# Retention attention into a SoLU block on one core: where q is transposed, how g_ln is loaded, and how the last 512 tokens are laid out

## The chip, the cores and the metric

The kernel runs on one core of one Trainium2 chip. The metric is the device time of one execution in microseconds (us), lower is better. The core has a matrix engine (PE, fed with weights by PEld), a vector engine (DVE), an activation engine (ACT), GpSimd (POOL) and a sync engine (SP) that only issues transfers. Sixteen DMA engines move data between HBM and the on-chip memory SBUF; matrix results land in the eight banks of PSUM.

## The reference

```python
kv  = einsum('bhsd,bhse->bhde', k, v)            # b=8, h=8, s=576, d=64: no softmax
o   = einsum('bhsd,bhde->bhse', q, kv)
o   = o / sqrt(mean(o*o, -1) + 1e-6) * g_norm    # norm over the 64 values of a head
x   = o.transpose(0, 2, 1, 3).reshape(4608, 512)
hid = x @ w_in                                   # 512 -> 1024
e   = exp(hid - max(hid));  u = hid * e / (sum(e) + 1e-9)
ln  = (u - mean(u)) / sqrt(var(u) + 1e-6) * g_ln # over the 1024 values of a token
out = ln @ w_out                                 # 1024 -> 512, float32
```

## The kernel before

The 4608 tokens are worked off in nine **chunks** of 512. Chunk c below 8 is the first 512 tokens of batch c; a partition p holds the four tokens 4p to 4p+3 (the groups j). Chunk 8 takes the last 64 tokens of all eight batches: partition 16b+p holds four tokens of batch b. Everything is computed with features on the partitions and tokens on the free axis, in bf16 where it feeds PE.

A chunk passes these steps. `kv_mm` (L272) makes k'v per head in a PSUM bank of the tag `misc`, four copies (L282 on DVE, L284 on ACT, one after the other) bring it to `kvd`. q is transposed to `qT`: in the chunks of `XBAR` by one DMA through the crossbar (`q_turn`, L302, issued by SP), in the others by 16 PE transposes in two halves (`qT_mm`, L292, also in a `misc` bank, of which there is one) with a DVE copy for each half (L297). `o_mm` (L317) gives the attention output in two halves of heads `hf`, each in two banks z. Each of the four pieces is squared (L332 on ACT; or copied by DVE, L324, and squared by L328), averaged per head by `s_mm` (L338), turned into 1/rms by a logarithm and an exponential (L342, L346), and multiplied in (`x_mul`, L353), which frees the `o` bank. Then eight tiles f of `h_mm` (L420, four matmuls each), each followed by the exponential `e` (L428), the product `u` (L435, which frees one of two `h` banks), its square `usq` (L444 on ACT, L446 on POOL) and the sums of pairs of `e` (`es`, L452 on POOL). `sums` (L484) adds u, u² and e over the features by PE, DVE transposes the result (L493), a small matmul (L498) and four small DVE instructions give the variance, two on ACT `rstd` (L518, L520). The mean of a token is taken out of `w_out` beforehand: `w_mean` (L526, eight matmuls in float32) and `w_center` (L532, eight DVE instructions) make `w_out_sb` once, in chunk 0. Last, `out_mm` (L541, four groups m of eight matmuls), `scale` by rstd (L548, `ob`) and `store` (L557, 256 KB each).

POOL issues all loads (L210 k and v, L217 q, L223 the last tokens of q, L230, L233 the weights); these cast float32 to bf16 on the way. Three buffers each hold k, v and q, so loads run up to three chunks ahead. SP issues the small loads at the start, the crossbar transposes and the stores; the last chunk's odd stores go out from ACT's queue. `warm` (L186) is a set of matmuls on zeros between the first real ones.

The order on every engine is made at build time by `Plan.order`: each step has an engine, an assumed length, a rank and what it needs; again and again the step that could start first goes next, the rank breaks ties. Each engine then works strictly in that order, waiting by semaphore. Numbers in `plan.add` thus set an order and no times.

Of the kernel before, what the change touches and what calls it, by code (L numbers as in the profile page):

```python
# [84 lines left out]
def kernel(  # L85
# [20 lines left out]
    nc = tc.nc  # L106
# [13 lines left out]
    XBAR = tuple(range(3, NC))  # L120
# [11 lines left out]
    COPIED = (0,)  # L132
# [15 lines left out]
    nc.sync.dma_start(g_ln_sb[:, :], moe_g_ln.rearrange("(n p) -> p n", p=128))  # L148

    ident = big.tile([128, 128], BF16, name="ident")  # L150
    fold = big.tile([128, 32], FP32, name="fold")
# [303 lines left out]
    for c in range(NC):  # L455
        for f in range(NF):
# [9 lines left out]
            engine = "act" if f in (2, 6) and c > 1 else "pool"  # L466
# [98 lines left out]
    for c in range(NC):  # L565
# [10 lines left out]
        for m in range(4):  # L576
# [7 lines left out]
            plan.add(("ob", c, m), "dve", 0.67, r + (2 * m + 2) / 8, lambda c=c, m=m: scale(c, m),  # L584
# [36 lines left out]
```

## Time and profile before

| | |
|---|---|
| median of 3 runs | 211.62 us (210.85 to 212.26) |
| the profiled execution | 212.84 us |
| its span, first to last instruction | 211.1 us |
| PE, DVE, ACT, POOL busy | 186.9, 128.5, 133.0, 135.5 us |
| mean granted clock of PE | 0.971 of full speed |

The profile is of one execution; its views are a page of sums, windows (busy time of each engine in a stretch), the chain that ended last, and a timeline of single instructions. A time in brackets at a row's end is the idle time of that engine just before, with what ended it. Starts are exact; the ends of matmuls are modelled, so PE work is best measured from start to start.

### The profile page before, as it was taken

The numbers are of one execution on the slowest core, as the hardware profiler recorded it, in microseconds if no ns is written. First come the engines' busy times: TensorE is split into PE (matmuls) and PEld (weight loads), VectorE is DVE, ScalarE is ACT, GpSimd is POOL, SyncE is SP. The second block draws the span as 40 slices with busy tenths as digits, with TensorE's granted clock in tenths as the row PEclk, the third lists the DMA queues.
The fourth block names the chain that finished last, engine by engine and source line by source line (L and its number), as shares of the span: only waits on it lengthen the run. The fifth ranks groups of instructions, "written<-read, shape, count | busy, mean of one in ns | idle before, by whom it ended". The sixth has DMA issues, their size and how long they took to land.

```text
span 211.1 us, 4084 instructions
## 1 busy us (share of the span) xinstructions
PE 186.9 (89%) x1614; PEld 83.2 (39%) x1614; DVE 128.5 (61%) x243; ACT 133.0 (63%) x231; POOL 135.5 (64%) x142
## 2 busy tenths in 40 slices
PE   7499897889948999999999999999999999999900
PEld 2243442543412435435444443543444444444300
DVE  1444567579860759667676866858666577663420
ACT  2046599456842877969779796976978585353100
POOL 7772389994380788696796966569385568586000
PEclk9999999999995999999999999999999999999995
DMA  4999999999999239979999997662121022022042
GB/s 47 163 203 205 199 373 227 200 202 203 193 123 237 64 33 195 242 121 148 237 176 128 212 248 112 204 107 104 50 102 50 25 78 90 14 97 101 0 115 83
DMA packets 43058, 30.14 MB, mean 143 GB/s; under 512 B 14880, under 2 KB 37408, under 8 KB 43040
## 3 DMA queue, kind: packets, MB, share of 16 engines
q0 software_dynamic: 24208, 17.30, 54.2%
q1 hardware_dynamic: 18560, 12.07, 22.4%
q10 hardware_dynamic: 272, 0.52, 0.8%
q8 instruction: 12, 0.20, 0.4%
q14 instruction: 6, 0.05, 0.1%
HBM read 32.51 MB, written 9.44 MB: 199 GB/s over the span
## 4 chain that ended last, share of the span: by engine, by line
PE 64%; DMA 25%; DVE 3%; issue 1%; ACT 1%; POOL 0%; DVEq 0%; POOLq 0%
PE out_ps L541 27%; PE h_ps L420 24%; DMA q_sb<-in_q_dram 9%; DMA v_sb<-in_v_dram 7%; DMA qT_sb<-q_sb 6%; PE misc_ps L484 5%; DMA k_sb<-in_k_dram 3%; PE s_ps L338 3%; PE o_ps L317 2%; DVE w_out_sb L532 2%; PE misc_ps L272 2%; PE misc_ps L498 1%; DVE ob_sb L548 1%; PE misc_ps L292 1%; POOL q_sb L217 0%
## 5 line engine op out<-in xcount | busy, mean ns | idle before, releaser
L420 PE MATMUL h_ps<-x_sb,w_in_sb 128*128 128x512 bf16 x288 | 74.7, 383 | 0.5 <-DVE u_sb L435 0.4
L541 PE MATMUL out_ps<-w_out_sb,u_sb 128*128 128x512 bf16 x272 | 70.6, 384 | 0.4 <-DVE w_out_sb L532 0.3
L452 POOL TENSOR_TENSOR es_sb<-e_sb 128x512 bf16<-128x512 f32 x36 | 45.8, 1272 | 36.5 <-ACT e_sb L428 36.3
L446 POOL TENSOR_TENSOR usq_sb<-u_sb 128x512 bf16<-128x512 bf16 x58 | 59.9, 1038 | 13.7 <-DVE u_sb L435 9.2
L435 DVE TENSOR_TENSOR u_sb<-h_ps,e_sb 128x512 bf16<-128x512 f32 x72 | 49.4, 687 | 31.6 <-ACT e_sb L428 30.9
L428 ACT ACTIVATE e_sb<-h_ps,zero_t 128x512 f32<-128x512 f32 x72 | 49.3, 684 | 21.2 <-PE h_ps L420 20.8
L541 PEld LDWEIGHTS <-u_sb 128*128 128x128 bf16 x288 | 27.2, 99 | 34.9 <-issue 5.6
L420 PEld LDWEIGHTS <-w_in_sb 128*128 128x128 bf16 x288 | 27.2, 98 | 34.5 <-issue 5.4
L548 DVE TENSOR_SCALAR ob_sb<-out_ps,rstd 128x512 f32<-128x512 f32 x34 | 25.2, 745 | 10.7 <-PE out_ps L541 6.8
L332 ACT ACTIVATE osq_sb<-o_ps,zero_t 128x512 bf16<-128x512 f32 x31 | 19.7, 682 | 14.6 <-PE o_ps L317 14.5
L353 DVE SCALAR_TENSOR_TENSOR x_sb<-o_ps,g_rep,rst_sb 128x512 bf16<-128x512 f32 x32 | 23.9, 747 | 7.8 <-ACT rst_sb L346 7.8
L346 ACT ACTIVATE rst_sb<-lss_sb,zero_t 128x512 f32<-128x512 f32 x36 | 26.1, 725 | 0.6
L342 ACT ACTIVATE lss_sb<-s_ps,eps_t 128x512 f32<-128x512 f32 x34 | 23.4, 688 | 1.5 <-PE s_ps L338 1.3
L284 ACT CAST kvd<-misc_ps 64x256 bf16<-64x256 f32 (+1 forms) x20 | 6.5, 325 | 14.6 <-DVE kvd L282 13.9
L338 PE MATMUL s_ps<-osq_sb,head_mean 128*128 128x512 bf16 x34 | 13.2, 388 | 0.9 <-ACT lss_sb L342 0.5
L186 PE MATMUL s_ps<-zeros 128*128 128x512 bf16 x39 | 11.6, 427 | 1.5 <-DVE zeros L153 1.2
L317 PE MATMUL o_ps<-qT_sb,kvd 64*64 64x32 bf16 (+1 forms) x240 | 7.7, 232 | 4.2 <-DMA qT_sb<-q_sb 4.1
L444 ACT ACTIVATE usq_sb<-u_sb,zero_t 128x512 bf16<-128x512 bf16 x14 | 10.1, 720 | 0.9 <-DVE u_sb L435 0.9
L217 POOL DMA_DIRECT2D q_sb<-in_q_dram x10 | 8.7, 872 | 2.2 <-DMA v_sb<-in_v_dram 1.4
L272 PE MATMUL misc_ps<-v_sb,k_sb 96*64 96x64 bf16 x384 | 8.0, 197 | 2.1 <-DMA v_sb<-in_v_dram 2.1
L210 POOL DMA_DIRECT2D k_sb<-in_k_dram x10 | 7.6, 760 | 3.3 <-DMA w_in_sb<-in_moe_w_in_dram 2.7
L518 ACT ACTIVATE lv<-vare,zero_t 128x4 f32<-128x4 f32 x9 | 2.7, 297 | 10.9 <-DVE vare L514 10.9
(60 smaller groups left out, 123.8 us busy)
## 6 DMA issues: line engine op xcount, KB each, us to landing
out_dram<-ob_sb SPq DMA_DIRECT2D x34, 256.0 KB, 3.1
k_sb<-in_k_dram POOLq DMA_DIRECT2D x6, 576.0 KB, 9.0
v_sb<-in_v_dram POOLq DMA_DIRECT2D x6, 576.0 KB, 12.5
q_sb<-in_q_dram POOLq DMA_DIRECT2D x6, 512.0 KB, 15.0
w_out_f<-in_moe_w_out_dram POOLq DMA_DIRECT2D x1, 2048.0 KB, 18.1
k_sb<-in_k_dram POOLq DMA_DIRECT2D x4, 288.0 KB, 11.0
v_sb<-in_v_dram POOLq DMA_DIRECT2D x4, 288.0 KB, 11.4
q_sb<-in_q_dram POOLq DMA_DIRECT2D x4, 256.0 KB, 10.5
```

The source lines that it names most:

```text
L332: nc.scalar.activation(out=t[:, :], in_=T[("o", *i)].rearrange("p a b c -> p (a b c)"), func=AF.Square, bias=zero_t[:, :])
L338: nc.tensor.matmul(t[:, :], head_mean[:, :], T["osq", i][:, :], start=True, stop=True)
L342: nc.scalar.activation(out=t[:, :], in_=T["s", i][:, :], func=AF.Ln, bias=eps_t[:, :])
L346: nc.scalar.activation(out=t.rearrange("p a b c -> p (a b c)"), in_=T["lss", i][:, :], func=AF.Exp, scale=-0.5, bias=zero_t[:, :])
L353: nc.vector.scalar_tensor_tensor(out=T["x", c][:, 2 * hf:2 * hf + 2, z], in0=T["o", c, hf, z][:, :, :, :], scalar=g_rep[:, :], in1=T["rst" ...
L420: nc.tensor.matmul(t[:, :], w_in_sb[:, dt, f * 128:(f + 1) * 128], T["x", c][:, dt].rearrange("p a b c -> p (a b c)"), start=(dt == 0), st ...
L428: nc.scalar.activation(out=T["e", c, f // 2][:, f % 2, :], in_=T["h", c, f][:, :], func=AF.Exp, bias=zero_t[:, :])
L435: nc.vector.tensor_tensor(out=T["u", c][:, f, :], in0=T["h", c, f][:, :], in1=T["e", c, f // 2][:, f % 2, :], op=MUL)
L446: nc.gpsimd.tensor_tensor(out=dst, in0=src, in1=src, op=MUL)
L452: nc.gpsimd.tensor_tensor(out=T["es", c][:, n, :], in0=e[:, 0, :], in1=e[:, 1, :], op=ADD)
L541: nc.tensor.matmul(T["acc", c, m][:, :], T["u", c][:, f, m * 128:(m + 1) * 128], w_out_sb[:, f, :], start=(f == 0), stop=(f == NF - 1),)
L548: nc.vector.tensor_scalar_mul(out=t[:, :], in0=T["acc", c, m][:, :], scalar1=T["rstd", c][:, m:m + 1])
```

## The change

Six edits stand in it. The crossbar takes chunks 4 to 8, so that chunk 3 goes by PE and DVE. g_ln (1024 floats) is loaded as eight rows of 128 and turned by one PE transpose, where it was loaded as 128 columns of eight single floats. In chunk 8 the partition is 8p+b in place of 16b+p: the load of the last q, the columns in `o_mm` and the pattern of the stores follow. Of the squares that go by a copy, chunk 0 keeps one (first half) and chunk 1 gets two, all three on POOL now. In chunk 8, ACT takes five of the eight u² and two of the four last scales. The warm matmuls go from 54 to 40. The planner's table changes with it.

```diff
-    XBAR = tuple(range(3, NC))
+    XBAR = tuple(range(4, NC))
...
-    COPIED = (0,)
+    COPIED = ((0, 0), (1, 0), (1, 1))
...
-    nc.sync.dma_start(g_ln_sb[:, :], moe_g_ln.rearrange("(n p) -> p n", p=128))
+    g_rows = big.tile([NF, 128], FP32, name="g_rows")
+    nc.sync.dma_start(g_rows[:, :], moe_g_ln.rearrange("(n p) -> n p", p=128))
...
+    def turn_g():
+        t = T["g_ps"] = bank(("misc", "g"), [128, NF], FP32)
+        nc.tensor.transpose(t[:, :], g_rows[:, :], eye[:NF, :NF])
+
     def make_g_mean():
+        nc.vector.tensor_copy(g_ln_sb[:, :], T["g_ps"][:, :])
...
-    for n in range(9):
-        plan.add(("warm", "s", n), "pe", 0.65, 8.0, lambda: warm(3), ["warm"], first=[("s", "warm", n)])
-    for n, key in enumerate((("o_mm", 0, 1), ("s_mm", (0, 0, 0)), ("s_mm", (0, 1, 0)), ("s_mm", (0, 0, 1)), ("s_mm", (0, 1, 1)))):
-        plan.add(("warm", n), "pe", 0.7, -9.0, lambda: warm(3, "misc"), [key], first=[("misc", "warm", n)])
+    for n in range(8):
+        plan.add(("warm", "s", n), "pe", 0.45, 8.0, lambda: warm(2), ["warm"], first=[("s", "warm", n)])
+    for n, key in enumerate((("o_mm", 0, 0), ("s_mm", (0, 0, 0)), ("o_mm", 0, 1), ("s_mm", (0, 1, 0)))):
+        plan.add(("warm", n), "pe", 0.65, 7.0, lambda: warm(3, "misc"), [key], first=[("misc", "warm", n)])
...
-            q_last[16 * b:16 * b + 16].rearrange("p h j d -> p h (j d)"),
+            q_last[b:128:B].rearrange("p h j d -> p h (j d)"),
...
-                cols = slice(0, 128) if c < B else slice(16 * b, 16 * b + 16)
+                cols = slice(0, 128) if c < B else slice(b, 128, B)
...
-        (nc.vector if i[1] else nc.gpsimd).tensor_tensor(out=t[:, :], in0=T["oc", i][:, :], in1=T["oc", i][:, :], op=MUL)
+        nc.gpsimd.tensor_tensor(out=t[:, :], in0=T["oc", i][:, :], in1=T["oc", i][:, :], op=MUL)
...
-            engine = "act" if f in (2, 6) and c > 1 else "pool"
+            engine = "act" if f in ((2, 6) if c < NC - 1 else (1, 3, 5, 6, 7)) and c > 1 else "pool"
...
-        nc.vector.tensor_scalar_mul(out=t[:, :], in0=T["acc", c, m][:, :], scalar1=T["rstd", c][:, m:m + 1])
+        if c == NC - 1 and m % 2:
+            nc.scalar.activation(out=t[:, :], in_=T["acc", c, m][:, :], func=AF.Copy, scale=T["rstd", c][:, m:m + 1])
+        else:
+            nc.vector.tensor_scalar_mul(out=t[:, :], in0=T["acc", c, m][:, :], scalar1=T["rstd", c][:, m:m + 1])
...
-            dst = out.rearrange("(b s) d -> b s d", b=B)[:, 512:S, :].rearrange("b (p j) d -> j b p d", j=4)
+            dst = out.rearrange("(b s) d -> b s d", b=B)[:, 512:S, :].rearrange("b (p j) d -> j p b d", j=4)
```

The order moves at three places that matter below. The first is DVE in chunk 2, around `w_center`; `x_sb_747` (before) and `x_sb_745` (changed) are the pieces of chunk 2, `u_sb_624` and `u_sb_573` those of chunk 1. Before:

```order
L435 TENSOR_TENSOR u_sb_624<-h_ps_630,e_sb_572 128x512
L297 COPY qT_sb_659<-misc_ps_641 128x1024
L532 SCALAR_TENSOR_TENSOR w_out_sb_69<-w_out_f_68,g_ln_sb_73,out_ps_555 128x512 x2
L297 COPY qT_sb_659<-misc_ps_670 128x1024
L532 SCALAR_TENSOR_TENSOR w_out_sb_69<-w_out_f_68,g_ln_sb_73,out_ps_555 128x512 x6
L353 SCALAR_TENSOR_TENSOR x_sb_747<-o_ps_681,g_rep_72,rst_sb_737 128x2x256
L493 STREAM_TRANSPOSE sumT_sb_753<-misc_ps_697 128x512
L353 SCALAR_TENSOR_TENSOR x_sb_747<-o_ps_682,g_rep_72,rst_sb_745 128x2x256
L435 TENSOR_TENSOR u_sb_624<-h_ps_652,e_sb_666 128x512
```

The same place on DVE in the changed kernel:

```order
L306 COPY qT_sb_651<-misc_ps_639 128x1024
L444 TENSOR_TENSOR u_sb_573<-h_ps_631,e_sb_648 128x512
L541 SCALAR_TENSOR_TENSOR w_out_sb_69<-w_out_f_68,g_ln_sb_73,out_ps_547 128x512
L306 COPY qT_sb_651<-misc_ps_663 128x1024
L541 SCALAR_TENSOR_TENSOR w_out_sb_69<-w_out_f_68,g_ln_sb_73,out_ps_547 128x512 x5
L362 SCALAR_TENSOR_TENSOR x_sb_745<-o_ps_675,g_rep_72,rst_sb_727 128x2x256
L541 SCALAR_TENSOR_TENSOR w_out_sb_69<-w_out_f_68,g_ln_sb_73,out_ps_547 128x512 x2
L362 SCALAR_TENSOR_TENSOR x_sb_745<-o_ps_676,g_rep_72,rst_sb_741 128x2x256
L502 STREAM_TRANSPOSE sumT_sb_758<-misc_ps_699 128x512
```

Both pieces of x now stand ahead of the transpose of the sums, one of them between the last two `w_center` and the rest. The second place is DVE a little later, where chunk 3 begins (the `CAST` to `kvd_70` are its kv copies). Before:

```order
L353 SCALAR_TENSOR_TENSOR x_sb_747<-o_ps_769,g_rep_72,rst_sb_861 128x2x256
L282 CAST kvd_70<-misc_ps_798 64x256 x2
L435 TENSOR_TENSOR u_sb_624<-h_ps_856,e_sb_877 128x512
L353 SCALAR_TENSOR_TENSOR x_sb_747<-o_ps_770,g_rep_72,rst_sb_889 128x2x256
L435 TENSOR_TENSOR u_sb_624<-h_ps_883,e_sb_877 128x512
L548 TENSOR_SCALAR ob_sb_907<-out_ps_872,rstd_849 128x512
L435 TENSOR_TENSOR u_sb_624<-h_ps_898,e_sb_919 128x512
```

The same place on DVE in the changed kernel:

```order
L362 SCALAR_TENSOR_TENSOR x_sb_745<-o_ps_760,g_rep_72,rst_sb_856 128x2x256
L291 CAST kvd_70<-misc_ps_807 64x256 x2
L560 TENSOR_SCALAR ob_sb_880<-out_ps_771,rstd_805 128x512
L362 SCALAR_TENSOR_TENSOR x_sb_745<-o_ps_761,g_rep_72,rst_sb_882 128x2x256
L306 COPY qT_sb_901<-misc_ps_884 128x1024
L444 TENSOR_TENSOR u_sb_573<-h_ps_875,e_sb_721 128x512
L560 TENSOR_SCALAR ob_sb_909<-out_ps_865,rstd_805 128x512
L306 COPY qT_sb_901<-misc_ps_911 128x1024
```

Two copies to `qT_sb_901`, chunk 3's, have come in between. The third place is the end of ACT's program. Before:

```order
L428 ACTIVATE e_sb_2748<-h_ps_2752,zero_t_83 128x512
L518 ACTIVATE lv_2832<-vare_2830,zero_t_83 128x4
L520 ACTIVATE rstd_2834<-lv_2832,zero_t_83 128x4
L557 DMA out_0_dram<-ob_sb_2847 8x16x512
L557 DMA out_0_dram<-ob_sb_2853 8x16x512
```

The end of ACT's program in the changed kernel:

```order
L453 ACTIVATE usq_sb_2641<-u_sb_2639,zero_t_85 128x512
L527 ACTIVATE lv_2842<-vare_2840,zero_t_85 128x4
L529 ACTIVATE rstd_2844<-lv_2842,zero_t_85 128x4
L558 ACTIVATE ob_sb_2852<-out_ps_2819,rstd_2844 128x512
L569 DMA out_0_dram<-ob_sb_2852 16x8x512
L558 ACTIVATE ob_sb_2868<-o_ps_2854,rstd_2844 128x512
L569 DMA out_0_dram<-ob_sb_2868 16x8x512
```

ACT scales two of the four last results itself and issues their stores, whose pattern now begins with 16 in place of 8. On SP the first crossbar transpose, chunk 3's, falls away, and the next one (chunk 4) stands between the second and the third store as before. On PE 16 transposes come in ahead of chunk 3's `o_mm`, and the last `sums` stands four `out` matmuls earlier. From the second `sums` to the last chunk the order on all engines is nearly the one before.

## Rows read from the trace of the kernel before

**Rows 1.** The page: busy time by engine; PE's granted clock in 40 slices (tenths).

```profile
PE 186.9 (89%) x1614; PEld 83.2 (39%) x1614; DVE 128.5 (61%) x243; ACT 133.0 (63%) x231; POOL 135.5 (64%) x142
...
PEclk9999999999995999999999999999999999999995
```

**Rows 2.** The chain that ended last: start, length, what (us).

```profile
51.41 12.79 DMA qT_sb<-q_sb
64.23 0.64 PE o_ps L317 x8
...
69.93 0.86 PE h_ps L420 x4
...
84.72 0.34 PE o_ps L317 x8
...
87.97 0.86 PE h_ps L420 x4
```

**Rows 3.** Windows: stretch, its length, busy time (instructions) by engine, clock, DMA.

```profile
core 0: us, PE busy (x) PEld busy (x) DVE busy (x) ACT busy (x) POOL busy (x), PEclk, DMA share, GB/s
23.60:43.30 19.70, 16.14 (x162) 7.92 (x155) 12.02 (x22) 14.84 (x28) 16.81 (x17) 1.00 1.35 254
43.30:60.20 16.90, 15.81 (x157) 7.44 (x157) 15.12 (x28) 12.03 (x21) 9.38 (x11) 1.00 1.35 196
60.20:64.20 4.00, 0.00 (x0) 0.00 (x0) 1.86 (x4) 0.69 (x1) 3.15 (x3) 0.77 1.20 125
64.20:69.20 5.00, 4.97 (x19) 1.84 (x20) 0.04 (x1) 2.02 (x4) 0.00 (x0) 0.50 0.82 203
```

**Rows 4.** Timeline of PE: q transposes of chunk 2, `o_mm` of chunk 3.

```profile
43.30 0.62 PE L292 MATMUL misc_ps<-ident,q_sb 128*128 128x128 bf16 x8 [0.57 <-DMA q_sb<-in_q_dram]
...
45.80 0.61 PE L292 MATMUL misc_ps<-ident,q_sb 128*128 128x128 bf16 x8
...
64.23 0.64 PE L317 MATMUL o_ps<-qT_sb,kvd 64*64 64x256 bf16 x8 [4.07 <-DMA qT_sb<-q_sb]
```

**Rows 5.** Timeline of DVE and POOL, single instructions of the fill.

```profile
12.78 0.68 DVE L324 COPY oc_sb<-o_ps 128x512 f32<-128x512 f32 x1
...
13.93 1.05 POOL L328 TENSOR_TENSOR osq_sb<-oc_sb 128x512 bf16<-128x512 f32 x1
...
41.51 2.03 POOL L446 TENSOR_TENSOR usq_sb<-u_sb 128x512 bf16<-128x512 bf16 x2
...
46.44 0.69 DVE L297 COPY qT_sb<-misc_ps 128x1024 bf16<-128x1024 bf16 x1 [0.17 <-PE misc_ps L292]
...
47.05 4.03 DVE L532 SCALAR_TENSOR_TENSOR w_out_sb<-w_out_f,g_ln_sb,out_ps 128x512 bf16<-128x512 f32 x6
```

**Rows 6.** Windows as in rows 3: start, an ordinary store, the last stores, the end.

```profile
4.50:7.50 3.00, 2.12 (x16) 1.01 (x15) 0.78 (x2) 0.00 (x0) 3.00 (x5) 1.00 1.08 115
7.50:14.30 6.80, 4.97 (x54) 2.10 (x53) 3.42 (x9) 1.79 (x4) 4.03 (x7) 1.00 1.31 194
194.00:194.50 0.50, 0.50 (x4) 0.24 (x3) 0.00 (x0) 0.00 (x0) 0.50 (x1) 1.00 0.98 377
203.50:204.00 0.50, 0.00 (x0) 0.00 (x0) 0.00 (x0) 0.00 (x0) 0.00 (x0) 1.00 0.53 193
209.60:211.10 1.50, 0.00 (x0) 0.00 (x0) 0.00 (x0) 0.00 (x0) 0.00 (x0) 0.50 0.00 0
```

**Rows 7.** Timeline of the last instructions on PE, DVE and ACT's queue.

```profile
197.90 2.76 PE L541 MATMUL o_ps<-w_out_sb,u_sb 128*128 128x512 bf16 x12
...
200.64 1.40 DVE L548 TENSOR_SCALAR ob_sb<-o_ps,rstd 128x512 f32<-128x512 f32 x2
...
200.75 1.94 ACTq L557 DMA_DIRECT2D out_dram<-ob_sb  x2
```

**Rows 8.** DMA issues of 190 to 196 us: median us from issue to landing.

```profile
out_dram<-ob_sb SPq DMA_DIRECT2D x2, 256.0 KB, 2.3
```

**Rows 9.** Timeline of PE: one half of chunk 8's `o_mm`.

```profile
155.82 0.69 PE L317 MATMUL o_ps<-qT_sb,kvd 64*64 64x32 bf16 x64
```

More of the change, by code (lines that the diff above doesn't have):

```diff
@@ L147 @@
     nc.sync.dma_start(g_rep[64:128, :], g_norm[:, None])
-    nc.sync.dma_start(g_ln_sb[:, :], moe_g_ln.rearrange("(n p) -> p n", p=128))
+    g_rows = big.tile([NF, 128], FP32, name="g_rows")
+    nc.sync.dma_start(g_rows[:, :], moe_g_ln.rearrange("(n p) -> n p", p=128))
     ident = big.tile([128, 128], BF16, name="ident")
+    eye = big.tile([NF, NF], FP32, name="eye")
     fold = big.tile([128, 32], FP32, name="fold")
@@ L177, in make_g_mean @@
         )
-    plan.add("g_mean", "dve", 1.2, 0.1, make_g_mean)
+    plan.add("turn_g", "pe", 0.2, -1.9, turn_g, ["ident"], first=[("misc", "g")])
+    plan.add("g_mean", "dve", 0.95, 0.1, make_g_mean, ["turn_g"], uses=[("misc", "g")])
     def warm(n, tag="s"):
@@ L188 @@
     plan.add("warm", "pe", 5.2, -9.0, lambda: warm(12), first=[("s", "warm")])
-    for n in range(9):
-        plan.add(("warm", "s", n), "pe", 0.65, 8.0, lambda: warm(3), ["warm"], first=[("s", "warm", n)])
-    for n, key in enumerate((("o_mm", 0, 1), ("s_mm", (0, 0, 0)), ("s_mm", (0, 1, 0)), ("s_mm", (0, 0, 1)), ("s_mm", (0, 1, 1)))):
-        plan.add(("warm", n), "pe", 0.7, -9.0, lambda: warm(3, "misc"), [key], first=[("misc", "warm", n)])
+    for n in range(8):
+        plan.add(("warm", "s", n), "pe", 0.45, 8.0, lambda: warm(2), ["warm"], first=[("s", "warm", n)])
+    for n, key in enumerate((("o_mm", 0, 0), ("s_mm", (0, 0, 0)), ("o_mm", 0, 1), ("s_mm", (0, 1, 0)))):
+        plan.add(("warm", n), "pe", 0.65, 7.0, lambda: warm(3, "misc"), [key], first=[("misc", "warm", n)])
     def make_ident():
         make_identity(nc, ident)
+        make_identity(nc, eye)
     def make_fold():
@@ L395 @@
                 rz = r + w * (0.4 + 0.5 * hf + 0.12 * z)
-                if c in COPIED and z:
+                if (c, hf) in COPIED and z:
                     plan.add(("oc", i), "dve", 0.62, rz, lambda i=i: o_copy(*i), [("o_mm", c, hf)],
                              uses=[(tag, *i)], first=[("oc", i)])
-                    plan.add(("sq", i), "dve" if hf else "pool", 0.62 if hf else 1.3, rz + 0.01, lambda i=i: o_sq_copy(*i), [("oc", i)],
+                    plan.add(("sq", i), "pool", 1.05, rz + 0.01, lambda i=i: o_sq_copy(*i), [("oc", i)],
                              uses=[("oc", i)], first=[("osq", i)])
@@ L583 @@
                          uses=[("u", c)] + ([(tag, c, m)] if half else []), first=[] if half else [(tag, c, m)])
-            plan.add(("ob", c, m), "dve", 0.67, r + (2 * m + 2) / 8, lambda c=c, m=m: scale(c, m),
+            plan.add(("ob", c, m), "act" if c == NC - 1 and m % 2 else "dve", 0.67, r + (2 * m + 2) / 8, lambda c=c, m=m: scale(c, m),
                      [("out", c, m, 1), ("rstd", c)], uses=[(tag, c, m)], first=[("ob", c, m)])
```

## The prediction

> **What bounds the kernel now.** I read the page first. PE is busy for 186.9 of 211.1 us, and the row of its granted clock has one dip ahead of the end, in the 13th of 40 slices, at 63 to 69 us [rows 1]. So PE is the bound, but not everywhere, and the question is where it waits. The chain that ended last answers: from about 70 us to 199 us it is PE work without a break, and what interrupts PE is ahead of that and behind it [rows 2]. There are three places.
>
> The first is the stall of chunk 3. SP issues its crossbar transpose at 51.41 us, as soon as q has landed, and it takes 12.79 us, since the loads of chunk 4 run beside it [rows 2]. PE has nothing else in its order and idles for 4.07 us [rows 4]. PE's clock goes down in this idle time (mean 0.77, then 0.50, that is 1.2 of 2.4 GHz) and stays down to about 69 us [rows 3]. Its price is read off the chain: the same five groups (`o_mm`, out, h, s, out) take 69.93 - 64.23 = 5.70 us there and 87.97 - 84.72 = 3.25 us at full clock, an excess of 2.45 us [rows 2].
>
> The second is the fill, up to 60 us. In its later part, 43.3 to 60.2 us, DVE is the fullest engine but for PE: 15.12 of 16.90 us, with PE at 15.81 [rows 3]. In the earlier part no engine is full: PE 16.14, POOL 16.81, ACT 14.84 of 19.70 us [rows 3].
>
> The third is the end. DVE makes the last two scaled tiles until 202.04 us, though PE was done at 200.66 [rows 7], and from 202.04 to the span's end at 211.1 us only the last stores run: 9.06 us, where a store in the steady part lands 2.3 us after its issue [rows 8]. In the windows the ordinary store keeps the DMA engines busy to 0.98 at 377 GB/s, the last four only to 0.53 at 193 GB/s [rows 6]: half of the sixteen engines do the work.
>
> **Part by part.** The sum is made against the profiled execution (212.84 us, span 211.1). It lies 1.2 us over the median of 211.62, and I carry the difference over to the median.
>
> *Crossbar from chunk 4.* The stall of 4.07 us and the slow stretch of 2.45 us go: -6.52. What comes in is 16 PE transposes in two halves, which took 0.62 and 0.61 us in chunk 2 [rows 4], on PE's path: +1.23. Two DVE copies of 0.69 us come too [rows 5]. They stand between the kv copies and the u of chunk 1, in the stretch where DVE is 89% full [rows 3]. I charge them in full, +1.38, since `out_mm` and `h_mm` wait for what is queued behind them (the scale that frees an `out` bank, the u that frees an `h` bank); the other end is 0, if DVE's remaining 1.78 us of idle time takes them up. Late next is chunk 4's transpose. Its q is issued at the same place, its transpose no longer shares the engines with another, and its `o_mm` stands some 20 us behind chunk 3's [rows 2], so I give it no wait.
>
> *g_ln as rows.* From 4.5 to 7.5 us the DMA engines move 115 GB/s, against 194 in the 6.8 us behind [rows 6]: (194 - 115) / 194 x 3.0 = 1.22 us of loading lost, in which I see the 1024 single floats. The loads run back to back until chunk 3's q, so all of them should come 1.2 us sooner. Yet I credit 0. The q transposes of chunk 2 do wait for a load, 0.57 us [rows 4], but in the new order the kv copies of chunk 2 stand behind a second u of chunk 1 and the last `w_mean` behind one more `h_mm`, and then DVE's eight `w_center` (six of them 4.03 us [rows 5]) and both pieces of x have to pass before the sums are turned. The bounds are -1.2 (all of it arrives) and +1.2 (the new order costs as much again).
>
> *Squares.* Chunk 1 takes two squares off ACT and gives DVE two copies of 0.68 us and POOL two squares of 1.05 us [rows 5]. In 23.6 to 43.3 us DVE has 7.7 us to spare and hides the copies; without that they would cost 1.36. POOL has 2.9 us to spare there; its last squares of chunk 0 end at 43.54 us [rows 5], and the sums that read them come after chunk 2's second half of q is transposed (45.80 [rows 4]), so 2.1 us more just fit. Counted at 0.
>
> *Fewer warm matmuls, ACT's squares in chunk 8.* Both are off the path: the first are fillers, the second moves POOL work to an ACT with room. 0, but see the second rival.
>
> *The last stores.* The pattern of a last store begins with 8 before and 16 now; the ordinary one begins with 128. The rows bound it: at the share of 0.53 nothing is gained, at the share of 0.98 a store takes the ordinary 2.3 us from issue, and behind the last packet 1.5 us pass to the span's end [rows 6, 8]. So 9.06 us become at best 3.8: -5.26, or 0. I take the full gain, because half the share at 8 goes with all of it at 16. The Trainium skill, "DMA: Bandwidth & Descriptors", on why a DMA increments its semaphore by 16, says that the number of engines is the largest up to 16 that divides the slowest dimension of both sides. By it 8 becomes 16 and the term is -5.26; the share of 0.53 agrees, and no run here shows a pattern that begins with 16.
>
> *The last scales.* Two of four go to ACT; the last one can start when PE ends (200.66) and takes the 0.70 us of a DVE scale [rows 7], so it ends at 201.36 and not 202.04: -0.68. The sums stand one group of matmuls earlier, which moves PE work behind them and takes none away.
>
> *Columns of chunk 8.* `o_mm` reads and writes every eighth column now. 64 matmuls take 0.69 us [rows 9], two halves. The number stays the same, so no gain; if each took twice as long it would be +1.4. I take +0.2, near the row. The Trainium skill, "Advanced Engine Details and Errata", section on memory cachelines, speaks against this edit: a non-contiguous PSUM pattern slows matmuls significantly, and SBUF wants at least two hits on a line of 16 bytes, where eight bf16 columns are one line. It has no price; no run so far shows it.
>
> The sum is -6.52 + 1.23 + 1.38 - 5.26 - 0.68 + 0.2 = -9.65 us. From the median this gives 211.62 - 9.65 = 202.0 us (a profiled span near 201.4).
>
> **The rivals.** *The start's gain arrives.* The 1.2 us of loads and the 1.38 us of copies both come out in favour: 202.0 - 2.6 = 199.4 us. For it speaks that ACT, 14.84 of 19.70 us busy, loses two squares in the fill; against it the DVE row of the later part.
>
> *The clock goes down once more.* In the new order PE stands at the `out` matmuls that follow `w_center` one by one and then waits for a piece of x, around 50 to 53 us, and the warm matmuls ahead of the first `h_mm` are fewer. One more slow stretch costs what the old one did: 202.0 + 2.45 = 204.4 us. Against it: at the same pace of `w_center` the clock held before (1.00 in 43.3 to 60.2 us [rows 3]).
>
> *The stores stay on eight engines.* If the order of the partitions doesn't change how a store is spread, the edit doesn't do its work: 202.0 + 5.26 = 207.2 us.
>
> *Strided columns cost.* By the rule on cachelines, at twice the time of each matmul, 202.0 + 1.2 = 203.2 us.
>
> *Slower.* With fewer warm matmuls the clock could stay at half through the fill. PE's 16.14 us in 23.6 to 43.3 us [rows 3] would be 32.3, which is 12.6 over the stretch: 202.0 + 12.6 = 214.6 us. Each us at the low clock costs 2 x 0.82 - 1 = 0.64 us there, so it decides from about 15 us on. Against it: PE is 82% busy in that stretch, at clock 1.00, and no matmul of it is a warm one.
>
> **How the numbers follow.** Forecast 0.45 (200.8 to 203.2); the start's gain 0.2; clock 0.17; stores 0.08; strided 0.05; slower 0.02; 0.03 for what I don't see. The range, 199.0 to 205.2 us, holds the forecast, the start's gain, the clock and the strided case, and leaves out the stores on eight engines, the slow fill and the rest. A difference of 1%, 2.1 us, is about what a measurement of this kernel can tell from no change. All cases but the slow fill and part of the unseen are faster by more: 0.95; within 1% 0.03; slower 0.02.
>
> **What would show it.** No wait of PE for `qT` around 60 us and clock 1.00 in that slice; two more qT copies in a DVE without gaps from 44 to 62 us; chunk 4's first `o_mm` near 81 us in place of 84.72 [rows 2]; a DMA rate near 194 GB/s from 4.5 us on; last stores at a share near 1 and landing about 2.3 us after issue, with the span ending 4 us behind the last scale. The forecast is wrong if PE waits elsewhere by as much, if the share at the end stays at 0.5, or if the start's 1.2 us comes through whole.

## The result, and the profile after

The changed kernel takes 202.31 us (median of 4 runs, 202.24 to 202.42), and the kernel before 211.73 (also four runs); the ratio is 0.956 (95% interval 0.9527 to 0.9593). The profiled execution took 202.24 us, its span is 200.5. The prediction was 202.0 us in a range of 199.0 to 205.2.

Two lines of the page answer to [rows 1]: the busy time of the engines, and PE's granted clock in 40 slices.

```profile
PE 184.0 (92%) x1617; PEld 82.8 (41%) x1617; DVE 128.5 (64%) x244; ACT 135.6 (68%) x235; POOL 135.0 (67%) x143
...
PEclk9999999999999999999999999999999999999999
```

The windows answer to [rows 3] and to the start in [rows 6]: stretch, length, busy time (instructions) by engine, clock, DMA share, GB/s.

```profile
4.50:7.50 3.00, 2.94 (x17) 1.29 (x15) 1.29 (x4) 0.00 (x0) 3.00 (x5) 1.00 1.24 168
7.50:14.30 6.80, 5.26 (x78) 2.52 (x77) 2.81 (x6) 1.73 (x4) 5.31 (x7) 1.00 1.29 195
...
43.30:60.20 16.90, 15.46 (x161) 7.24 (x159) 15.34 (x28) 10.94 (x20) 10.32 (x11) 1.00 1.24 196
60.20:64.20 4.00, 4.00 (x32) 1.96 (x30) 2.37 (x5) 3.56 (x6) 2.25 (x3) 1.00 0.85 183
64.20:69.20 5.00, 5.00 (x39) 2.02 (x38) 3.85 (x7) 2.89 (x5) 4.61 (x5) 1.00 0.35 90
```

From 60.2 to 64.2 us PE was idle before and works all the time now; the stretch behind it is at clock 1.00 and not 0.50. The start moves 168 GB/s in place of 115. The timeline of PE shows the middle, and the chain that ended last names what came before it:

```profile
40.28 0.95 PE L281 MATMUL misc_ps<-v_sb,k_sb 96*64 96x64 bf16 x48 [1.24 <-DMA v_sb<-in_v_dram]
...
58.13 0.61 PE L301 MATMUL misc_ps<-ident,q_sb 128*128 128x128 bf16 x8
...
60.30 0.61 PE L301 MATMUL misc_ps<-ident,q_sb 128*128 128x128 bf16 x8
60.84 0.41 PE L326 MATMUL o_ps<-qT_sb,kvd 64*64 64x256 bf16 x8
...
67.77 0.62 PE L493 MATMUL misc_ps<-u_sb,stat_sel 128*32 128x512 bf16 x8
```

```profile
20.70 19.54 DMA v_sb<-in_v_dram
...
79.03 0.34 PE o_ps L326 x8
```

The transposes of chunk 3's q stand in the old stall, and `o_mm` follows without a wait for qT. Chunk 4's first `o_mm` comes at 79.03 us, 5.7 us sooner than in [rows 2]. But the chain has a new member: `kv_mm` of chunk 2 waits 1.24 us for v, which lands at 20.70 + 19.54 = 40.24 us. In the profile of before the same `kv_mm` starts at 40.25 and waits 0.17:

```profile
40.25 0.95 PE L272 MATMUL misc_ps<-v_sb,k_sb 96*64 96x64 bf16 x48 [0.17 <-DMA v_sb<-in_v_dram]
...
73.53 0.62 PE L484 MATMUL misc_ps<-u_sb,stat_sel 128*32 128x512 bf16 x8
```

So up to 40 us nothing is won. At the end (timelines of PE, ACT and ACT's queue, then two windows), against [rows 7] and [rows 6]:

```profile
192.57 2.75 PE L550 MATMUL o_ps<-w_out_sb,u_sb 128*128 128x512 bf16 x12
193.12 0.69 ACT L558 ACTIVATE ob_sb<-out_ps,rstd 128x512 f32<-128x512 f32 x1
...
195.37 0.69 ACT L558 ACTIVATE ob_sb<-o_ps,rstd 128x512 f32<-128x512 f32 x1 [1.56 <-PE o_ps L550]
196.08 0.56 ACTq L569 DMA_DIRECT2D out_dram<-ob_sb  x1
```

```profile
195.00:198.90 3.90, 0.33 (x2) 0.00 (x0) 0.00 (x0) 0.69 (x1) 0.00 (x0) 1.00 0.88 269
198.90:200.50 1.60, 0.00 (x0) 0.00 (x0) 0.00 (x0) 0.00 (x0) 0.00 (x0) 0.96 0.00 0
```

PE ends at 195.32 us and the span 5.18 us later; before it was 200.66 and 10.44 us. The stores run at a share of 0.88, and the last lands 2.8 us behind its issue (196.08 to 198.90).

The two spans differ by 10.6 us, and four distances hold it all: up to `kv_mm` of chunk 2 +0.03; from there to the second sums 33.28 to 27.49, so -5.79; from there to PE's end 127.13 to 127.55, so +0.42; and the tail -5.26.

In e3, e4, e10 and e11 below the median takes in one or two slow executions (205.6 to 210.4 us), which the ratio leaves out.

### The profile page after: what moved, and what is told of

It is laid out like the page before. It is cut to its first block, busy times and chain, and to the rows that moved or that the text cites. A ratio compares the mean times of both kernels' runs of the same rounds, so it can differ in the third digit from the quotient of the medians.

```text
span 200.5 us, 4103 instructions
## 1 busy us (share of the span) xinstructions
PE 184.0 (92%) x1617; PEld 82.8 (41%) x1617; DVE 128.5 (64%) x244; ACT 135.6 (68%) x235; POOL 135.0 (67%) x143
## 4 chain that ended last, share of the span: by engine, by line
PE 73%; DMA 16%; DVE 3%; POOL 3%; issue 1%; ACT 1%; POOLq 0%
PE out_ps L550 29%; PE h_ps L429 26%; DMA v_sb<-in_v_dram 10%; DMA k_sb<-in_k_dram 6%; PE misc_ps L493 5%; PE s_ps L347 3%; PE o_ps L326 3%; PE misc_ps L281 3%; DVE w_out_sb L541 2%; PE o_ps L550 2%; PE misc_ps L301 1%; PE misc_ps L507 1%; POOL q_sb L226 1%; POOL w_in_sb L239 1%; DVE x_sb L362 1%
## 5 line engine op out<-in xcount | busy, mean ns | idle before, releaser
L550 PE MATMUL out_ps<-w_out_sb,u_sb 128*128 128x512 bf16 x272 | 69.7, 380 | 1.2 <-DVE w_out_sb L541 1.2
L455 POOL TENSOR_TENSOR usq_sb<-u_sb 128x512 bf16<-128x512 bf16 x55 | 56.8, 1040 | 14.6 <-DVE u_sb L444 14.2
L560 DVE TENSOR_SCALAR ob_sb<-out_ps,rstd 128x512 f32<-128x512 f32 x33 | 24.6, 745 | 10.6 <-PE out_ps L550 6.2
L341 ACT ACTIVATE osq_sb<-o_ps,zero_t 128x512 bf16<-128x512 f32 x30 | 19.2, 682 | 10.4 <-PE o_ps L326 10.4
L453 ACT ACTIVATE usq_sb<-u_sb,zero_t 128x512 bf16<-128x512 bf16 x17 | 12.2, 720 | 3.9 <-DVE u_sb L444 3.9
L291 DVE CAST kvd<-misc_ps 64x256 bf16<-64x256 f32 (+1 forms) x20 | 7.2, 362 | 6.9 <-PE misc_ps L281 4.1
L194 PE MATMUL s_ps<-zeros 128*128 128x512 bf16 x28 | 9.8, 476 | 1.4 <-DVE zeros L155 1.2
L219 POOL DMA_DIRECT2D k_sb<-in_k_dram x10 | 8.1, 807 | 2.3 <-DMA w_in_sb<-in_moe_w_in_dram 1.7
L281 PEld LDWEIGHTS <-k_sb 96*64 96x64 bf16 x384 | 7.0, 112 | 6.1 <-issue 6.1
```

The costliest lines, as they stand in the source:

```text
L281: nc.tensor.matmul(t[hh * 64:hh * 64 + 64, n, :], T["k", b][:, h, i, :], T["v", b][:, h, i, :], start=(n == 0 and i == 0), stop=(i == 5), ...
L341: nc.scalar.activation(out=t[:, :], in_=T[("o", *i)].rearrange("p a b c -> p (a b c)"), func=AF.Square, bias=zero_t[:, :])
L455: nc.gpsimd.tensor_tensor(out=dst, in0=src, in1=src, op=MUL)
L550: nc.tensor.matmul(T["acc", c, m][:, :], T["u", c][:, f, m * 128:(m + 1) * 128], w_out_sb[:, f, :], start=(f == 0), stop=(f == NF - 1),)
```

## The experiments

Each is an edit of the changed kernel, and its ratio is to the kernel before on the same chip. The distances are of one profile for each run. The chips and executions scatter more than those of the result did (the kernel before took 209.7 to 214.3 us), so the distances in the profiles carry the readings. Columns: median; ratio with interval; start of chunk 2's `kv_mm`; from there to the second sums; from PE's end to the span's end (us).

| run | median | ratio | `kv_mm` | to sums | tail |
|---|---|---|---|---|---|
| e1_xbar3 | 207.13 | 0.973 (0.9682 to 0.9778) | 40.44 | 32.47 | 5.12 |
| e2_layout_old | 206.29 | 0.9705 (0.9655 to 0.9755) | 40.33 | 27.69 | 9.37 |
| e3_write_strided | 203.17 | 0.9522 (0.947 to 0.9574) | 41.31 | 27.53 | 5.16 |
| e4_g_columns | 203.32 | 0.9554 (0.9499 to 0.961) | 40.57 | 28.89 | 5.18 |
| e5_after_again | 202.53 | 0.9551 (0.9503 to 0.9598) | 41.51 | 27.54 | 5.0 |
| e6_warm_old | 203.56 | 0.9597 (0.9561 to 0.9634) | 39.49 | 29.21 | 5.15 |
| e7_copies_act | 202.21 | 0.9539 (0.9498 to 0.958) | 40.35 | 27.49 | 5.1 |
| e8_squares_old | 203.13 | 0.9579 (0.954 to 0.9617) | 40.87 | 27.86 | 5.11 |
| e9_fillers | 202.39 | 0.9546 (0.9496 to 0.9595) | 40.64 | 27.49 | 5.12 |
| e10_scales_dve | 202.5 | 0.9549 (0.9496 to 0.9602) | 41.04 | 27.49 | 5.12 |
| e11_store_rows | 201.99 | 0.9538 (0.9482 to 0.9594) | 39.35 | 27.50 | 5.0 |
| e12_combined | 201.31 | 0.9469 (0.9431 to 0.9506) | 39.90 | 27.49 | 5.2 |

**e1_xbar3.**

```diff
-    XBAR = tuple(range(4, NC))
+    XBAR = tuple(range(3, NC))
```

> The changed kernel with chunk 3 turned by the crossbar again; all other edits stay. Theory (the gain of the middle is the stall and the slow stretch that the crossbar of chunk 3 made): PE waits some 4 us for qT near 60 us, the granted clock falls to 0.5 behind it, the second sums of PE come at 73 to 74 us in place of 67.8, and the time is 202.3 + 5.3 = 207.6 us (206.3 to 209.0). Rival (the other edits filled the gap: new order of the fill, g_ln as rows, the squares): the time stays under 204.5 us and the clock holds.

The chain, PE's timeline and a window of this run:

```profile
51.58 12.68 DMA qT_sb<-q_sb
```

```profile
64.30 0.41 PE L326 MATMUL o_ps<-qT_sb,kvd 64*64 64x256 bf16 x8 [4.11 <-DMA qT_sb<-q_sb]
```

```profile
64.20:69.20 5.00, 4.90 (x22) 1.91 (x22) 0.22 (x1) 2.20 (x4) 0.17 (x1) 0.66 1.22 188
```

Stall and slow clock (0.66 in the mean of the window) are back, with every other edit in place: 32.47 us to the second sums, 4.98 more than with PE transposes. The median is 4.6 us above that of e5. The rival falls.

**e2_layout_old.**

```diff
-            q_last[b:128:B].rearrange("p h j d -> p h (j d)"),
+            q_last[16 * b:16 * b + 16].rearrange("p h j d -> p h (j d)"),
...
-                cols = slice(0, 128) if c < B else slice(b, 128, B)
+                cols = slice(0, 128) if c < B else slice(16 * b, 16 * b + 16)
...
-            dst = out.rearrange("(b s) d -> b s d", b=B)[:, 512:S, :].rearrange("b (p j) d -> j p b d", j=4)
+            dst = out.rearrange("(b s) d -> b s d", b=B)[:, 512:S, :].rearrange("b (p j) d -> j b p d", j=4)
```

> The changed kernel with chunk 8's partitions ordered by sequence again (16 b + p), so plain columns and a store pattern that begins with 8. Theory (spread over sixteen engines is worth some 5.2 us, and strided columns cost 0.45 us in each of two halves of o_mm): the share at the end is 0.53 again, one half of o_mm takes 0.62 us from its start to the next start in place of 1.07, and the time is 202.3 + 5.2 - 0.9 = 206.6 us (205.5 to 207.6). Rival (the tail became shorter by the earlier sums and the scales on two engines, not by the spread): under 204.0 us. Second rival (the strided columns are hidden beside other work): 207.5 us.

A window at the end of this run, and one half of its `o_mm` with what follows:

```profile
196.00:198.00 2.00, 0.00 (x0) 0.00 (x0) 0.00 (x0) 0.00 (x0) 0.00 (x0) 1.00 0.50 164
```

```profile
150.39 0.69 PE L326 MATMUL o_ps<-qT_sb,kvd 64*64 64x32 bf16 x64
151.01 1.04 PE L550 MATMUL out_ps<-w_out_sb,u_sb 128*128 128x512 bf16 x4
```

The share is 0.50 again and the tail 9.37 us, 4.19 more. The earlier sums and the second engine for the scales are still there, so the spread alone brings 4.19. `o_mm` takes 0.62 us a half.

**e3_write_strided.**

```diff
-            q_last[b:128:B].rearrange("p h j d -> p h (j d)"),
+            q_last[16 * b:16 * b + 16].rearrange("p h j d -> p h (j d)"),
...
-                            T["qT", c][rows, 4 * hf + 2 * pp + hh, :, cols], start=True, stop=True,
+                            T["qT", c][rows, 4 * hf + 2 * pp + hh, :, cols if c < B else slice(16 * b, 16 * b + 16)], start=True, stop=True,
```

> The changed kernel with q_last loaded as before (16 b + p) and qT read by plain columns, while o_mm still writes every eighth column of PSUM; everything behind o_mm, the stores too, stays as changed. If the read of the moving operand is what costs: one half of o_mm takes 0.62 us start to start in place of 1.07, and the time is 202.3 - 0.9 = 201.4 us. If the write to PSUM is what costs: 1.07 us and 202.3 us. If each costs a part: between the two. The tail is that of the changed kernel in all cases.

The changed kernel's half of `o_mm` and what follows it, and then this run's two halves:

```profile
150.14 1.14 PE L326 MATMUL o_ps<-qT_sb,kvd 64*64 64x32 bf16 x64
151.21 1.04 PE L550 MATMUL out_ps<-w_out_sb,u_sb 128*128 128x512 bf16 x4
```

```profile
151.21 0.71 PE L326 MATMUL o_ps<-qT_sb,kvd 64*64 64x32 bf16 x64
151.85 1.04 PE L550 MATMUL out_ps<-w_out_sb,u_sb 128*128 128x512 bf16 x4
...
160.88 0.71 PE L326 MATMUL o_ps<-qT_sb,kvd 64*64 64x32 bf16 x64
161.52 1.04 PE L429 MATMUL h_ps<-x_sb,w_in_sb 128*128 128x512 bf16 x4
162.89 0.38 PE L347 MATMUL s_ps<-osq_sb,head_mean 128*128 128x512 bf16 x1 [0.33 <-ACT osq_sb L341]
```

From start to start a half takes 1.07 us with both sides strided and 0.64 with a strided write alone: the read costs 0.43, the write 0.02 over the 0.62 of plain columns. Behind the second half PE now waits 0.33 us for ACT's square, which the longer `o_mm` had covered, so only some 0.35 of the 0.9 us is won: from the first half to the sums of chunk 7 it is 174.64 - 151.21 = 23.43 us, with both sides strided 173.92 - 150.14 = 23.78. A ratio whose interval is 1 us to each side can't show it, and this profile started `kv_mm` 1.03 us later.

**e4_g_columns.** g_ln is loaded in columns, and `turn_g`, its copy and the second identity are gone.

```diff
-    g_rows = big.tile([NF, 128], FP32, name="g_rows")
-    nc.sync.dma_start(g_rows[:, :], moe_g_ln.rearrange("(n p) -> n p", p=128))
+    nc.sync.dma_start(g_ln_sb[:, :], moe_g_ln.rearrange("(n p) -> p n", p=128))
```

> The changed kernel with g_ln loaded as single floats in columns again, without the transpose on PE and the second identity. Theory (the loads come 1 us later up to w_out, but what they feed is late for other reasons by 43 us): 202.3 us, within 0.5. Rival (the start's gain does reach the end): 202.3 + 1.2 = 203.5 us. Second rival (the transpose and the second identity cost more than the loads give): 201.6 us or less.

The ratio is that of the changed kernel, but its interval is some 1.2 us to each side, so the times alone don't exclude the first rival. The chain shows that v of chunk 2 is issued 1.46 us later than in the changed kernel's profile and lands 0.3 us later, at 40.53:

```profile
22.16 18.37 DMA v_sb<-in_v_dram
```

The profile shows something else too, in windows:

```profile
52.00:54.00 2.00, 1.86 (x12) 0.61 (x12) 2.00 (x5) 0.82 (x2) 0.02 (x1) 0.85 1.22 184
54.00:56.00 2.00, 2.00 (x13) 0.64 (x12) 1.00 (x5) 0.94 (x2) 2.00 (x2) 0.50 1.31 199
56.00:58.00 2.00, 2.00 (x52) 1.10 (x51) 1.26 (x2) 1.31 (x5) 0.01 (x1) 0.80 1.32 200
```

The clock falls to 0.50 just behind the `out` matmuls that wait for `w_center`, the place that the prediction's second rival names, and the way to the second sums is 28.89 us: 1.40 more.

**e5_after_again.** No edit.

> The changed kernel without an edit, timed on the chip of this call, since the four experiments so far showed a granted clock below 1.00 in stretches of the fill where the changed kernel's own profile had none. If those dips belong to the edits: 202.3 us in each execution and clock 1.00. If they belong to the changed kernel, in some executions and not in others: 202.3 us where the clock holds, 203 to 205 us where it falls at 22 to 28 us or at 52 to 58 us, and a mean granted clock of 0.975 to 0.99 in those.

Six executions took 201.34 to 203.87 us, with mean clocks of 0.999 and 0.977 at these ends. The dips belong to the changed kernel, in some executions. In this profile:

```profile
12.00:14.00 2.00, 1.64 (x12) 0.47 (x11) 1.16 (x2) 0.51 (x1) 0.67 (x1) 0.50 1.28 204
24.00:26.00 2.00, 2.00 (x30) 0.97 (x29) 0.86 (x3) 1.21 (x3) 0.00 (x0) 0.68 1.36 201
26.00:28.00 2.00, 1.83 (x11) 1.23 (x11) 0.96 (x2) 0.69 (x1) 1.51 (x2) 0.50 1.33 341
```

```profile
41.51 0.95 PE L281 MATMUL misc_ps<-v_sb,k_sb 96*64 96x64 bf16 x48
```

`kv_mm` starts at 41.51 us without a wait: here PE is late and not v, which was issued at 21.31 us and took 18.4, so it had landed near 39.7. These dips cost some 1.8 us. From there on the pace is that of the others.

**e6_warm_old.** The table of warm matmuls as before the change.

```diff
-    for n in range(8):
-        plan.add(("warm", "s", n), "pe", 0.45, 8.0, lambda: warm(2), ["warm"], first=[("s", "warm", n)])
+    for n in range(9):
+        plan.add(("warm", "s", n), "pe", 0.65, 8.0, lambda: warm(3), ["warm"], first=[("s", "warm", n)])
```

> The changed kernel with the table of warm matmuls as it was before the change (54 in place of 40). Theory (the fewer warm matmuls leave PE idle for 1.7 us around 20 to 22 us, and the clock falls behind it in some executions): clock 1.00 from 5 to 40 us, and the time is that of the changed kernel where its clock holds, 202.3 us, with a narrower spread. Rival (the number of warm matmuls does nothing for the clock): dips as in the changed kernel and the same times. Second rival (warm matmuls stand ahead of real work): 0.5 to 1.0 us slower than the changed kernel on this chip.

The clock is 1.00 through the fill and the spread 202.94 to 204.03 us, as the theory says; but the median is 1.0 above e5. The loss is not ahead of real work, as the second rival has it: `kv_mm` starts at 39.49. The table changes the order behind it, where PE now waits for the copies of chunk 3 (0.81 of the 1.72 us by which the way to the second sums is longer; the rest is not traced):

```profile
57.34 0.61 PE L301 MATMUL misc_ps<-ident,q_sb 128*128 128x128 bf16 x8 [0.81 <-DVE kvd L291]
```

**e7_copies_act.**

```diff
-        nc.vector.tensor_copy(T["qT", c][:, 4 * hf:4 * hf + 4], T["qTp", c, hf][:, :, :, :])
+        (nc.scalar.copy if c == 3 else nc.vector.tensor_copy)(T["qT", c][:, 4 * hf:4 * hf + 4], T["qTp", c, hf][:, :, :, :])
```

> The changed kernel with the two qT copies of chunk 3 on ACT and not on DVE. The prediction charged these copies at 1.38 us in a full DVE. If that is so: the second sums of PE come 1.4 us sooner and the time is 1.4 us under the changed kernel on this chip. If the idle time of DVE takes them up: within 0.4 us of it. If ACT becomes what is late: slower by 0.5 us or more, with PE waiting for qT_sb from ACT or for exponentials behind the copies.

27.49 us to the second sums with the copies on ACT, and 27.49 with them on DVE. In both profiles PE works from 56.9 us to the second sums without a wait, so the copies cost it nothing on either engine.

**e8_squares_old.** `COPIED = (0,)`, chunk 1's squares all on ACT.

> The changed kernel with the squares of the first two chunks shared out as before the change (chunk 1 all on ACT; of chunk 0 one on POOL, one on DVE). The prediction counted the edit at 0. If that holds: within 0.4 us of the changed kernel on this chip. Rival (ACT is what is late in the fill, so two squares of 0.57 us count): 1.1 us slower. Second rival (the copies on DVE and the squares on POOL delay k and v of chunk 2 or 3, which POOL issues): 0.5 to 1.0 us faster.

0.6 us above e5, and 27.86 us to the second sums, so 0.37 of it behind `kv_mm`; the intervals overlap widely. Between 0 and 0.6 us, not settled further.

**e9_fillers.** More warm matmuls, and the order of real work kept.

```diff
+            if (c, f, dt) == (0, 0, 2): warm(6)
...
+            if (c, m, f) in ((0, 0, 6), (0, 0, 7)): warm(3 if f == 6 else 1)
```

> The changed kernel, its order of real work unchanged, with more warm matmuls in the places where PE was idle ahead of the dips: three in place of two in the eight fillers of the start, six inside the first h_mm ahead of the third piece of x, three and one inside the first out_mm ahead of its last two weights. Theory (the idle places let the clock fall, and the dips make the spread of 201.3 to 203.9 us): the clock is 1.00 from 5 us to the end of PE's work in the profile, the median is 201.5 us and no execution is above 202.3. Rival (the dips come from something else than PE's idle time): the same spread and a median of 202.5 us. Second rival (the fillers delay real work): spread narrow, but a median of 203 us as with the old table.

The profile has no dip, and the mean clocks are 0.992 to 1.000 (0.976 to 0.999 in e5). Yet the times are 201.15 to 203.06 us: a spread of 1.9 us, against 2.5 in e5. So the clock is not the only cause of it. A second one is in this row, the same as in the changed kernel's profile and longer:

```profile
40.64 0.95 PE L281 MATMUL misc_ps<-v_sb,k_sb 96*64 96x64 bf16 x48 [1.46 <-DMA v_sb<-in_v_dram]
```

A third lies outside the span: three of the six executions take 2.1 to 2.5 us more than their spans, the other three and all of e5 some 1.8.

**e10_scales_dve.** The four last scales all on DVE.

> The changed kernel with all four last scales on DVE; the stores stay on the same queues. The prediction's term: 0.68 us later, 203.2 us against 202.5 for the changed kernel on this chip. Rival (with the sums one group earlier the first three scales are done before PE's last matmul, so DVE is free for the last one as well): within 0.2 us in the profile's distance from PE's last matmul to the span's end, 5.2 us, and no change that the median can tell.

```profile
196.13 0.75 DVE L557 TENSOR_SCALAR ob_sb<-o_ps,rstd 128x512 f32<-128x512 f32 x1 [0.18 <-PE o_ps L550]
```

DVE waits for PE's last matmul and ends 0.80 us behind it, ACT in the changed kernel 0.74. The tail is 5.12 us: the second engine is worth nothing that the tail shows. The rival holds.

**e11_store_rows.** The rows of the last 256 KB stores lie 2 KB apart.

```diff
-            dst = out.rearrange("(b s) d -> b s d", b=B)[:, 512:S, :].rearrange("b (p j) d -> j p b d", j=4)
+            dst = out.rearrange("(b s) d -> b s d", b=B)[:, 512:S, :].rearrange("b (j p) d -> j p b d", j=4)
```

> The changed kernel with the rows of the last four stores put 2 KB apart in the output and not 8 KB (tokens of chunk 8 land in another order, so these rows of the output are permuted); sizes, queues, engines and everything ahead of the stores stay. Theory (the last stores run at 290 GB/s and not at 377 since rows that sixteen engines write at the same time lie badly in memory): some 370 GB/s at a share near 1 in the last stores, the last store lands 2.3 us behind its issue and not 2.9, and the tail is 0.6 to 0.9 us shorter. Rival (a store's first packets are slow wherever they go): share, rate and tail as in the changed kernel, within 0.2 us.

The windows show 363 GB/s in the second us of the stores and 289 in the third, where the changed kernel has much the same (356 and 277 from 196 us):

```profile
195.00:196.00 1.00, 0.00 (x0) 0.00 (x0) 0.00 (x0) 0.13 (x1) 0.00 (x0) 1.00 1.02 363
196.00:197.00 1.00, 0.00 (x0) 0.00 (x0) 0.00 (x0) 0.00 (x0) 0.00 (x0) 1.00 0.93 289
```

The spacing of the rows is not what costs. This profile has the earliest `kv_mm` of all, and the chain says why: v lands at 21.04 + 18.27 = 39.31 us.

```profile
21.04 18.27 DMA v_sb<-in_v_dram
39.35 0.96 PE misc_ps L281 x48
```

From there the pace is that of the others, so the second sums come 0.92 us sooner than in the changed kernel's profile (67.77):

```profile
66.85 0.61 PE L493 MATMUL misc_ps<-u_sb,stat_sel 128*32 128x512 bf16 x8
```

**e12_combined.** The fillers, e3's edit, and the last eighth of w_out behind q of chunk 2.

```diff
-        nc.gpsimd.dma_start(w_out_f[:, :, :], moe_w_out.rearrange("(n p) d -> p n d", p=128))
+        nc.gpsimd.dma_start(w_out_f[:, :7, :], moe_w_out.rearrange("(n p) d -> p n d", p=128)[:, :7])
...
+        if b == 2: nc.gpsimd.dma_start(w_out_f[:, 7:, :], moe_w_out.rearrange("(n p) d -> p n d", p=128)[:, 7:])
```

> The changed kernel, its order of work kept, with three edits together: the added warm matmuls of the fillers, the plain reads of qT in chunk 8 (o_mm still writes every eighth column), and the last eighth of w_out loaded behind q of chunk 2 in place of ahead of k. Theory (from the start of chunk 2's kv_mm every profile runs at the same pace, 27.5 us to the second sums, and that start is the landing of v of chunk 2, 39.3 to 41.0 us in the profiles so far): v lands some 0.8 us sooner, kv_mm starts at 39.0 to 40.2 us, chunk 8 is 0.35 us shorter, the clock holds, and the median is 201.2 us where the changed kernel had 202.5 (ratio near 0.949). Rival (something else is as late as v at 40 us, or the last w_mean now waits for its eighth): kv_mm of chunk 2 or the last w_mean waits for a DMA as long as before, and only chunk 8's 0.35 us is gained: 202.0 us.

201.31 us (200.97 to 202.08), the fastest of all, at a ratio of 0.9469 against 0.9551 for the changed kernel in e5, on another chip; the intervals just touch. `kv_mm` still waits, but less, and no w_mean waits for its eighth:

```profile
39.90 0.95 PE L281 MATMUL misc_ps<-v_sb,k_sb 96*64 96x64 bf16 x48 [0.66 <-DMA v_sb<-in_v_dram]
```

The three edits are not told apart. Chunk 8's 0.35 us is there (127.21 us from the second sums to PE's end, 127.55 in the changed kernel). But 39.90 lies among the starts of profiles without the moved load (39.35 to 41.51), so it is not shown that the order of the loads helps.

## Why the prediction was right, and where it was not

**Crossbar from chunk 4.** The mechanism is shown: e1 brings stall and slow clock back, and the clock holds in this stretch without them. The size was off. The terms -6.52, +1.23 and +1.38 make -3.91; from `kv_mm` of chunk 2 to the second sums it was -5.79, of which e1 shows 4.98 for the crossbar alone. The mis-sized term is the two DVE copies: "I charge them in full, +1.38", and e7 with PE's unbroken work shows 0. DVE was 89% full, but the fullness of a stretch did not say that anyone waited for the copies; the other end of the bound, 0, was the answer. The two transposes cost 0.45 and 0.54 us to the next start, 0.99 and not 1.23. Of what e1 leaves of the 5.79, 0.8 us, most is the slow stretch itself: 5.01 us for the five groups in e1 (64.30 to 69.31 in its chain), 5.70 before. The rows of e1 close the sum: its stall of 4.11 us and 5.01 - 3.25 = 1.76 for its slow stretch, less 0.99 for the transposes, make 4.88 of the 4.98, and no 1.38 is left over for the copies. Chunk 4's transpose got no wait, as forecast: issued at 60.00 us, it lands 4.4 us later, where chunk 3's took 12.79 beside the loads.

**g_ln as rows.** The value, 0, was right in the profile (`kv_mm` at 40.28 us, 40.25 before); the times of e4 fit it and are too coarse to confirm it. The reason failed. The prediction put the loss on copies of kv, `w_mean` and `w_center`; in fact the early loads did not hold their lead to v of chunk 2, for which PE waits: it is issued 1.1 us sooner (20.70 us against 21.81) and takes 19.5 us against 18.4. And what was said to swallow the gain doesn't: where v lands early, in e11, `kv_mm` starts 0.93 us sooner and the second sums come 0.92 sooner. v landed at 40.24 us here and at 39.31 in e11, with the same code up to there and the same bytes moved (263 and 264 GB/s from 28.0 to 39.3 us):

```profile
28.00:39.30 11.30, 8.78 (x49) 3.84 (x48) 8.42 (x14) 9.36 (x16) 11.27 (x12) 1.00 1.35 263
```

```profile
28.00:39.30 11.30, 8.94 (x50) 3.94 (x49) 8.04 (x14) 9.19 (x16) 11.27 (x13) 1.00 1.35 264
```

(The first row is of the changed kernel, the second of e11.) So the first rival, that the start's gain arrives, comes true in part in e11's profile, with 0.9 us. Why v lands later at the same total rate, these views don't show; it stays open.

**The last stores and the last scales.** -5.26 and -0.68 were forecast for the tail, and from PE's end it became 5.26 us shorter. The last scale now ends 0.74 us behind PE and not 1.38: -0.64, nearly the size forecast, but for another reason, and so by luck. A second engine brings nothing (e10, all on DVE: 0.80). Before, `rstd` came 1.35 us ahead of PE's end, and four scales in a row kept DVE busy past it; now it is there at 193.12 us, 2.2 us ahead, and three scales are done when PE ends. That is the work of the earlier sums, to which the prediction gave nothing; it is read off the rows, as no run puts the sums back. The first of the four scales before, and the last one in e2:

```profile
199.31 1.41 DVE L548 TENSOR_SCALAR ob_sb<-out_ps,rstd 128x512 f32<-128x512 f32 x2 [0.69 <-ACT rstd L520]
```

```profile
195.27 0.69 ACT L558 ACTIVATE ob_sb<-o_ps,rstd 128x512 f32<-128x512 f32 x1 [1.56 <-PE o_ps L550]
```

From the last scale's end to the span's end it was 9.06 us before, is 8.64 in e2 and 4.44 in the changed kernel. So the new pattern brings 4.20, where 5.26 was forecast, and 0.42 comes from what e2 shares with the changed kernel; that its first stores go out 1.5 us ahead of PE's end, where it was 0.6, may be the cause and is argued. The pattern brings less than forecast since a store lands 2.8 us behind its issue and not 2.3, at a share of 0.88 over the four; e11 rules out the spacing of the rows, and no run tells what it is. The Trainium skill, "DMA: Bandwidth & Descriptors", on why a DMA increments its semaphore by 16, made 16 engines of the new pattern: the share, 0.50 with a pattern that begins with 8 (e2) and 0.88 over all four stores with 16, agrees.

**Columns of chunk 8.** +0.2 was forecast; a half takes 0.45 us longer, and some 0.35 of the two halves' 0.9 reaches the end (e3; in e2, with plain columns on both sides, it is 127.21 us from the second sums to PE's end, 0.34 less). The rival of strided columns, at +1.2, was nearer for the instruction and not for the path. The Trainium skill, "Advanced Engine Details and Errata", on memory cachelines, speaks of both sides; here the strided SBUF read costs 0.43 us per 64 matmuls and the strided PSUM write 0.02, so for these matmuls the measurement agrees on the read and differs on the write.

**The clock.** The rival with 0.17 is real: not in the changed kernel's profile, but in e4's, at its place and with 1.40 us, and in the fill of e1 to e5, e8 and e10. Of the price forecast, 2.45 us, a little over half was paid. PE's two waits for `w_center` ahead of it, 0.94 and 0.28 us, are the same in the changed kernel's profile, where the clock holds, so they don't decide it alone. Nor does each dip cost time: of the four executions of the result two have a mean clock of 1.000 and two of 0.985 and 0.987, and all spans are 200.5 to 200.7 us. In e5 the dips cost what made PE later than v. With more warm matmuls (e6, e9, e12) no profile shows a dip in the fill, and no execution has a mean clock under 0.992; that PE's idle time makes the dips fits this and is not proved by it, since the profiles of e7 and e11 have none without them.

**The terms at 0.** For the squares e8 leaves 0 to 0.6 us open. For the fewer warm matmuls 0 holds on balance: the old table kept the clock and was 1.0 us slower (e6).

**The sum.** -9.65 us was forecast against the profiled execution, and it was -10.6 there. Part by part the middle won 1.88 us more than its terms, the tail 0.68 less, and the stretch between lost 0.42 where 0.2 was forecast. The number 202.0 came out near the measured 202.31 because two errors met: the terms were 1 us too small, and the execution that they were set against lay 1.2 us above the median of before, as the changed kernel's does not. That closeness is luck. What was not luck is the stall with its clock and the spread of the stores, which e1 and e2 take back one by one.

## What to carry to other kernels

When PE idles for a transfer, count the clock that goes with it: here the stall was 4.1 us and the slow stretch behind it 1.8 to 2.5. A busy share near 90% doesn't price an added instruction; find who waits for what is queued behind it. An earlier start is worth what the next transfer on the chain keeps of it: follow the landing of each load to the engine that waits. And a term that comes out at its forecast size can still have another cause: e10 took the second engine away, and the gain stayed.

## What was not expected of the hardware

- Executions of one kernel differed by 2.5 us (201.34 to 203.87 in e5), although from `kv_mm` of chunk 2 to the second sums eight profiles agree to within 0.05 us (27.49 to 27.54 in e3, e5, e7, e9 to e12 and the changed kernel). In these the scatter is made ahead of `kv_mm`, by v's landing and by the clock. It is not always so: e2 took 27.69 us, with a wait of 0.73 for q, and e4 28.89, with the clock at 0.50.
- 64 small matmuls pay 0.43 us for reading every eighth bf16 column of SBUF, and 0.02 for writing every eighth float of PSUM.
- Four stores that follow one another on all engines reached 373 GB/s in one half of a microsecond (196.5 to 197.0) and then fell to 275 to 291, so that their mean is 269; an ordinary one in the steady part showed 377 in its best half [rows 6]. The spacing of their rows in HBM made no difference.
